# Attention on one core: unnormalised exponentials, the reciprocal sums applied after the second product, two-bank score tiles and probability transposes one head pair later

## The chip, the cores and the metric

The kernel runs on 1 core of one Trainium2 chip. Five engines work side by side, each through its own queue in program order: TensorE (PE; its weight loads are listed apart as PEld), VectorE (DVE), ScalarE (ACT), GpSimd (POOL) and SyncE (SP), from which all transfers between HBM and SBUF are issued. TensorE writes only into PSUM, which has 8 banks; the other engines carry results from there to SBUF. The metric is the device time of one execution in microseconds.

## The reference

```python
scores = scale * np.matmul(q, k.transpose(0, 1, 3, 2))      # B, H, S, D = 4, 8, 576, 64
scores = np.where(causal, -1000000000.0, scores)
a = np.exp(scores - scores.max(-1, keepdims=True))
a /= a.sum(-1, keepdims=True) + 1e-09
local = np.matmul(a, v)
q_p = np.where(q > 0, q, np.exp(q) - 1.0) + 1.0
mem_out = (q_p @ M_prev) / (q_p @ z_prev + 1e-06)           # per head
g = 1.0 / (1.0 + np.exp(-beta))                             # one gate per head
x = g * mem_out + (1 - g) * local                           # -> 2304 tokens x 512
h = x @ w_in; sp = np.log1p(np.exp(h))
x = (h * np.tanh(sp)) @ w_out                               # 512 -> 2048 -> 512
out = ((x @ w1) * (x @ w2)) @ w3 @ w_out2                   # 512 -> 1024 -> 512
```

The change touches only the attention part, and what follows directly from where its buffers lie.

## The kernel before

Attention takes two heads at a time: 4 batches of 4 pairs are 16 pairs, and the loop at L487 makes 17 rounds, as each round works on pair `p` and finishes pair `p - 1`. The 576 query rows of a pair are cut into blocks of 128; block `ib` of 0 to 3 exists once for each head (`e` of 0 and 1), and the last 64 rows of both heads share one block of 128 (`s_last`, L365).

In one round, `s_blocks` (L359) multiplies `qt` by `kt` into PSUM bank A. The two heads lie on the upper and lower 64 partitions, so each product uses 64 rows of the array (the form is shown as 64*128). `maxed` (DVE, L352) adds the mask and finds the row maximum, and `expd` (ACT, L357) takes exponentials with their row sums. `normed` (L336) forms 1/sum and multiplies each block of exponentials by 1/sum and by 1 - g, half of the blocks on DVE and half on POOL (L347). `pt_g` (L401) transposes them in 7 groups of up to four 128x128 blocks through PSUM bank F, and ACT copies each group to SBUF (L407). `pv` (L410) then adds up in PSUM bank X the memory term (`M_` times the transposed `phi`) and the products of `v` with the transposed probabilities. Here each head fills 64 columns of the array (shown as 128*64). The sum is split into a rounded high part and a remainder (ACT L427, DVE L67) and kept in `xt` for the layers that follow.

`prep_qk` (L289) transposes q and k of the next pair (5 blocks each, L286) and copies them (L292). `prep_phi` (L304) computes the feature map, its norm with `z`, scales it by g/norm (POOL L326) and transposes it (5 blocks, L330 copies). Groups 1 and 0 of the transposes of a pair are written in its own round, the other five in the next.

The inputs of the layers hold 64-bit words, two 32-bit halves each, which `decode` (L91) turns into floats with six DVE instructions (L101 to L114) and one on POOL (L119) for a tile of 128x512; two more POOL instructions split it into high and low parts (L64, L67). In rounds 2 to 11 one such tile is decoded as background: eight for the first quarter of `w_in` and `w_out` (`lq0`) and two of `pre`. In the last round the first product of the layers, `emit_h((0, 0))`, is written between the end of the attention and the rest. It is followed by the loop at L627, unit after unit: `emit_h` (48 products of 384 columns), `emit_x2` of the unit before (48 more, which need `w_out`), and `split_y`. Every fp32 product shows as two matmul instructions of the same shape.

PSUM has 3 banks for A, 3 for X and 2 for F, each handed out singly, through attention and layers alike. The order of instructions within an engine is not the order of the source: a planner with a model of instruction times orders them (`schedule_with_timeline_sim`, L752) by source order and readiness. `tc.issue_after(i)` makes what it encloses queue behind `i` on the engine of `i`.

## Time and profile before

| what | value |
|---|---|
| median of 3 runs | 1037.71 us (1035.83 to 1039.62) |
| profiled execution | 1036.43 us, span 1034.6 us |
| mean granted TensorE clock | 0.998 |
| TensorE busy, weight loads busy | 98%, 82% of the span |
| DVE, ACT, POOL busy | 59%, 49%, 33% of the span |

The span runs from the first to the last instruction; the time of the execution has some 1.8 us around it. Attention takes the first quarter of the span, the layers the rest. A busy TensorE in this profile means that some matmul was under way: the matmuls are pipelined, and the end of each is modelled. What one really costs is read from the distance between the starts of two that follow each other. The chain of waits gives such distances directly, since it lists in order of time what the end waited for. Where two heads run on different halves of the array, their instructions start together.

### The profile page before, as it was taken

Reading aid. Unit: us, or ns where it says so; the run is one execution under the profiler, and the core shown is the slowest. Engines: PE = TensorE matmul, PEld = TensorE weight load, DVE = VectorE, ACT = ScalarE, POOL = GpSimd, SP = SyncE. Lnnn points to the kernel's source line nnn. Section 1 sums busy time; section 2 is a strip of 40 time slices with the busy share of each in tenths; the row PEclk is TensorE's granted clock in tenths of the full one; section 3 lists DMA queues with packets and bytes.
Section 4 is the critical chain, followed back from the end, with each engine's and each line's share of the span. In section 5 each row is a group of like instructions: output and inputs, shape, how many; then the busy total and the mean of one; then the engine's idle time right before and its main releaser. Section 6 shows DMA issues by size and latency. Waiting matters only on the chain.

```text
span 1034.6 us, 15072 instructions
## 1 busy us (share of the span) xinstructions
PE 1014.0 (98%) x5552; PEld 847.1 (82%) x5552; DVE 615.5 (59%) x1364; ACT 505.1 (49%) x1016; POOL 337.9 (33%) x345
## 2 busy tenths in 40 slices
PE   7999999999999999999999999999989999999998
PEld 4555656556799999999999999999768888888897
DVE  5999998865279765757576666668983121121111
ACT  4777768767546665555656545442323121221212
POOL 6776675651045434252434321112550000000000
PEclk9999999999999999999999999999999999999999
DMA  6434344310133233112312456222410010100101
GB/s 150 113 95 108 95 115 110 83 41 14 61 104 122 77 107 114 49 65 99 123 41 82 153 198 220 81 73 82 152 41 1 1 41 1 42 1 0 41 1 61
DMA packets 93626, 81.73 MB, mean 79 GB/s; under 512 B 68720, under 2 KB 72816, under 8 KB 93552
## 3 DMA queue, kind: packets, MB, share of 16 engines
q1 hardware_dynamic: 93552, 80.76, 25.2%
q8 instruction: 44, 0.72, 0.3%
q14 instruction: 30, 0.25, 0.1%
HBM read 65.54 MB, written 15.20 MB: 78 GB/s over the span
## 4 chain that ended last, share of the span: by engine, by line
PE 86%; DVE 6%; ACT 3%; SPq 2%; DMA 2%; issue 1%; POOL 1%; POOLq 0%; DVEq 0%; ACTq 0%
PE psX L61 34%; PE psA L61 29%; PE psF L61 16%; PE psF L405 5%; PE psX L286 2%; SPq L268 1%; ACT y L459 1%; DVE da L105 1%; PE psF L584 1%; DVE s L347 1%; ACT L456 0%; DMA draw<-in_moe_w_dram 0%; DVE da L103 0%; DVE gl L67 0%; DMA wft<-w_dram 0%
## 5 line engine op out<-in xcount | busy, mean ns | idle before, releaser
L119 POOL TENSOR_TENSOR da<-da,draw 128x512 f32<-128x512 f32 x72 | 104.1, 1455 | 331.4 <-DVE draw L114 255.9
L61 PE MATMUL psX<-gh,wqt 128*128 128x384 f32 x768 | 196.1, 335 | 0.2
L61 PEld LDWEIGHTS psX<-gh,wqt 128*128 128x128 f32 x768 | 138.6, 188 | 1.5 <-DVE y L463 0.5
L61 PE MATMUL psX<-gl,wqt 128*128 128x384 f32 x384 | 128.3, 335 | 1.1 <-DVE gl L67 1.1
L61 PE MATMUL psA<-xt,wqt 128*128 128x384 f32 x624 | 115.0, 336 | 1.4 <-DVE y L463 1.4
L61 PEld LDWEIGHTS psA<-xt,wqt 128*128 128x128 f32 x624 | 108.5, 188 | 3.2 <-DVE y L463 1.7
L357 ACT ACTIVATE s<-s,acc 128x384 f32<-128x384 f32 (+3 forms) x144 | 85.0, 595 | 37.5 <-DVE acc L352 21.1
L61 PE MATMUL psA<-x2h,w12t 128*128 128x512 f32 (+1 forms) x288 | 81.1, 357 | 2.9 <-POOL w12t L64 2.8
L61 PE MATMUL psX<-wft,room 128*128 128x512 f32 x336 | 82.6, 390 | 0.0
L352 DVE CUSTOM_DVE_ANT_0 s<-psA,mask 128x512 f32<-128x512 f32 (+2 forms) x144 | 65.0, 477 | 19.5 <-PE psA L61 16.9
L703 ACT COPY bs<-psA 128x512 f32<-128x512 f32 (+1 forms) x40 | 21.8, 544 | 112.3 <-PE psA L61 105.7
L61 PE MATMUL psX<-pt,raw 128*64 128x64 f32 (+4 forms) x576 | 75.0, 328 | 0.0
L61 PE MATMUL psA<-kt,qt 64*128 64x384 f32 (+3 forms) x256 | 71.1, 485 | 3.7 <-DVE acc L352 3.2
L61 PE MATMUL psF<-xt,wqt 128*128 128x384 f32 x408 | 73.9, 335 | 0.0
L61 PEld LDWEIGHTS psX<-gl,wqt 128*128 128x128 f32 x384 | 72.0, 188 | 1.8 <-DVE gl L67 1.4
L61 PEld LDWEIGHTS psX<-wft,room 128*128 128x128 f32 x336 | 62.6, 188 | 12.7
L407 ACT COPY pt<-psF 128x512 f32<-128x512 f32 (+1 forms) x112 | 59.0, 544 | 26.9 <-PE psF L405 23.4
L560 DVE TENSOR_TENSOR x<-x,psX 128x384 f32<-128x384 f32 x72 | 39.6, 549 | 54.1 <-PE psX L61 53.9
L61 PEld LDWEIGHTS psF<-xt,wqt 128*128 128x128 f32 x408 | 71.0, 188 | 0.1
L471 ACT CAST gh<-y 128x768 fp32r<-128x768 f32 x48 | 40.1, 837 | 57.6 <-PE psX L61 51.5
L61 PE MATMUL psA<-x2s,w12t 128*128 128x512 f32 x288 | 67.9, 389 | 0.0
L405 PEld LDWEIGHTS psF<-ident,s 128*128 128x128 f32 x400 | 45.3, 141 | 26.1 <-ACT phi L330 10.6
(117 smaller groups left out, 1938.9 us busy)
## 6 DMA issues: line engine op xcount, KB each, us to landing
draw<-in_moe_w_dram SPq DMA_DIRECT2D x32, 512.0 KB, 3.6
draw<-in_moe_w_out_dram SPq DMA_DIRECT2D x24, 512.0 KB, 4.0
draw<-in_moe_w_in_dram SPq DMA_DIRECT2D x16, 512.0 KB, 3.9
out_dram<-ob SPq DMA_DIRECT2D x18, 256.0 KB, 2.0
raw<-in_q_dram SPq DMA_DIRECT2D x32, 128.0 KB, 2.6
raw<-in_k_dram SPq DMA_DIRECT2D x32, 128.0 KB, 3.2
raw<-in_v_dram SPq DMA_DIRECT2D x32, 128.0 KB, 2.7
o_dram<-draw SPq DMA_DIRECT2D x8, 512.0 KB, 2.9
```

Source lines behind the costliest of these rows:

```text
L61: nc.tensor.matmul(o, lhsT=l, rhs=r, start=start, stop=stop)
L105: V.tensor_scalar(out=ai, in0=ai, scalar1=3, scalar2=0x3FFFFFF8, op0=ALU.logical_shift_left, op1=ALU.bitwise_and)
L119: nc.gpsimd.tensor_tensor(out=a, in0=a, in1=lw.bitcast(F32), op=ALU.add)
L268: dm(out=a[:, 0:4, e], in_=src[b, h0 + e, 0:512, :].rearrange("(i p) d -> p i d", p=128))
L286: nc.tensor.transpose(pt[:, x:x + 128], src[:, i].rearrange("p h d -> p (h d)"), ident)
L352: nc.vector.tensor_tensor_reduce(out=s, in0=o, in1=m, op0=ALU.add, op1=ALU.min, scale=-scale, scalar=init, accum_out=a,)
L357: nc.scalar.activation(out=s, in_=s, func=AF.Exp, scale=-1.0, bias=a, accum_out=r)
L405: nc.tensor.transpose(o[:, 128 * x:128 * x + 128], src[:, 128 * jb:128 * jb + 128], ident)
L407: nc.scalar.copy(out=t[:, 0:n], in_=o[:, 0:n])
L471: nc.scalar.copy(out=gh, in_=y[i])
L560: r = nc.vector.tensor_tensor(out=d, in0=d, in1=o, op=ALU.add)
L703: nc.scalar.copy(out=bs, in_=pb)
```

## The change

The exponentials are no longer normalised before they are transposed. 1 - g multiplies `v`, and g multiplies `M_prev` (`gate_v`, `gate_m`, on POOL). The feature map is scaled by (sum + 1e-9)/norm, so that every term of the sum in PSUM lacks the same factor 1/sum. 1/sum is spread over 64 columns, transposed on TensorE beside the feature map (`scale_phi`, `trans_phi`), and DVE multiplies the finished sums by it as it takes them out of PSUM. The split into high and low parts then works from SBUF, its subtraction on POOL.

A score tile now has two banks, one for each head, and there are two of them; X has two banks, F two. All seven groups of `pt_g` of a pair lie in the next round, three of them copied by DVE. The products of `pv` queue behind the last transpose of their pair. Blocks of q, k and phi are laid out so that four transposes serve 512 rows, and the last 64 rows of both heads go through small products with parts of an identity (`tails`, and two for q). z is loaded per batch, v by itself.

Background decoding in the attention rounds is by half tiles, one in each of rounds 3 to 10, which makes the four `w_in` tiles. The four `w_out` tiles of the first quarter are decoded in the last round, and no `pre` tile is in the attention. The PSUM pool of the attention is closed behind it, and the layers open a new one with the old sizes.

```diff
+    sk = ExitStack()
+    pool = [sk.enter_context(tc.tile_pool(name="ps0", bufs=1, space=PSUM))]
+    banks = {"X": 2, "F": 2}
...
 
     def psA():
-        return bank("A")
+        return pool[0].tile([128, 2, 512], F32, tag="A", name="psA", bufs=2)
...
+        for c in range(KD + KQ):
+            w, r0, c0 = (w_in, 128 * c, FQ * g) if c < KD else (w_out, FQ * g + 128 * (c - KD), 0)
+            for h in range(0, FQ, dec["w"]):
+                cs = slice(h, h + dec["w"])
+                yield words(w, r0, c0 + h), to_split(t[:, 0, c, cs], t[:, 1, c, cs])
...
+    decoder(at, 1, 1, WN // 2)
...
+    def gate_m(b):
+        for e, hv in enumerate((UP, DN)):
+            m = mr[b % 2][hv, :, e]
+            nc.gpsimd.tensor_tensor(
+                out=m, in0=m, in1=g_[hv, 1, e::2][:, :, None].to_broadcast([64, NP, D]), op=ALU.mult
+            )
...
+    def tails(o, src):
+        for e, hv in enumerate((UP, DN)):
+            mm(o[hv], src, ident[:, 64 * e:64 * e + 64], True, True)
...
+        d = st[p]
+        qt = ep.tile([128, 512], F32, tag="qt", name="qt", bufs=2)
+        kt = ep.tile([128, S], F32, tag="kt", name="kt", bufs=2)
+        for t, nm in ((qt, "q"), (kt, "k")):
+            o = psX()
+            trans4(o, d[nm])
+            nc.scalar.copy(out=t[:, 0:512], in_=o)
+            d[nm + "t"] = t
+        o = psX()
+        for e, hv in enumerate((UP, DN)):
+            mm(o[hv, 0:128], d["q"][:, 8], idh[:, e], True, True)
+        tails(o[:, 128:192], d["k"][:, 8])
+        t4 = ep.tile([128, 128], F32, tag="qd", name="qd", bufs=2)
+        nc.scalar.copy(out=t4, in_=o[:, 0:128])
+        nc.scalar.copy(out=kt[:, 512:S], in_=o[:, 128:192])
...
+        d["e"], d["dn"] = e, dn
+
+    def gate_v(p):
+        h0 = 2 * (p % NP)
+        a = st[p]["v"]
+        nc.gpsimd.tensor_tensor(
+            out=a, in0=a, in1=g_[:, 0:1, h0:h0 + 2, None].to_broadcast([128, NB, 2, D]), op=ALU.mult
         )
...
+    def scale_phi(p):
         d = st[p]
-        og = ogp[:, p % NP]
-        sl = slice(0, 8) if len(xs) > 1 else slice(8, 9)
-        rv = d["sum"][:, sl]
-        nc.vector.tensor_scalar(out=rv, in0=rv, scalar1=1e-9, scalar2=None, op0=ALU.add)
-        nc.vector.reciprocal(out=rv, in_=rv)
-        for ib, e in xs:
-            s = s4[:, 0:S] if ib == 4 else d["s"][ib, e]
-            x = 8 if ib == 4 else 2 * ib + e
-            (nc.gpsimd if x in ON_POOL else nc.vector).tensor_scalar(
-                out=s, in0=s, scalar1=d["sum"][:, x:x + 1], scalar2=og[:, x:x + 1], op0=ALU.mult, op1=ALU.mult
-            )
+        e, dn, sm = d["e"], d["dn"], d["sum"]
+        rb = ap_.tile([128, NC, D], F32, tag="phit", name="rb", bufs=1)
+        r = ap_.tile([128, NC], F32, tag="rs", name="rs", bufs=2)
+        nc.vector.scalar_tensor_tensor(out=dn, in0=sm, scalar=1e-9, in1=dn, op0=ALU.add, op1=ALU.mult)
+        nc.vector.tensor_scalar(out=r, in0=sm, scalar1=1e-9, scalar2=None, op0=ALU.add)
+        nc.vector.reciprocal(out=r, in_=r)
+        nc.gpsimd.tensor_tensor(out=e, in0=e, in1=dn[:, :, None].to_broadcast([128, NC, D]), op=ALU.mult)
+        nc.gpsimd.tensor_copy(out=rb[:, 0:8], in_=r[:, 0:8, None].to_broadcast([128, 8, D]))
+        d["r"], d["rb"] = r, rb
+
+    def trans_phi(p):
+        d = st[p]
+        e, r = d["e"], d["r"]
+        t = ap_.tile([128, 2, S], F32, tag="phi", name="phi", bufs=1)
+        for i, x in enumerate((e, d["rb"])):
+            o = psX()
+            trans4(o, x)
+            nc.scalar.copy(out=t[:, i, 0:512], in_=o)
+        o = psF()
+        tails(o[:, 0:64], e[:, 8])
+        tails(o[:, 64:128], r[:, 8:9].to_broadcast([128, D]))
+        nc.scalar.copy(out=t[:, :, 512:S], in_=o[:, 0:128].rearrange("p (i c) -> p i c", i=2))
+        d["phi"] = t
...
-        pt = [psA() for _ in range(2)]
+        pt = psA()
...
-                mm(pt[e][:, 256 * j:256 * j + W], d["qt"][r, 128 * ib:128 * ib + 128], d["kt"][r, 0:W], True, True)
+                mm(pt[:, e, 256 * j:256 * j + W], d["qt"][r, 128 * ib:128 * ib + 128], d["kt"][r, 0:W], True, True)
...
+        s = s4[p % 2][:, 0:S]
+        pt = psA()
         for z in range(2):
-            o = psA()[:, 0:CA]
+            mm(pt[:, z, 0:CA], d["q4"], d["kt"][:, CA * z:CA * z + CA], True, True)
+        for z in range(2):
+            o = pt[:, z, 0:CA]
             cs = slice(CA * z, CA * z + CA)
...
+    BY_VECTOR = (1, 3, 5)
...
+            d["last"] = nc.tensor.transpose(
+                o[:, 128 * x:128 * x + 128], src[:, 128 * jb:128 * jb + 128], ident
+            ).ins
             d.setdefault("t", {})[ib, e, jb] = t[:, 128 * x:128 * x + 128] if e is None else (t, 128 * x)
-        nc.scalar.copy(out=t[:, 0:n], in_=o[:, 0:n])
+        if gi in BY_VECTOR:
+            nc.vector.tensor_copy(out=t[:, 0:n], in_=o[:, 0:n])
+        else:
+            nc.scalar.copy(out=t[:, 0:n], in_=o[:, 0:n])
...
-        pm, pl = psX(), psX()[:, 0:64]
...
+        pm, pl = psX(), psF()[:, 0:64]
...
+        with tc.issue_after(d["last"]):
+            mm(pm, M_.rearrange("p e d -> p (e d)"), F[:, 0:512], True, False)
+            for jb in range(4):
+                for e in range(2):
...
+        xs = ap_.tile([128, S], F32, tag="xsum", name="xsum", bufs=1)
+        nc.vector.tensor_tensor(out=xs[:, 0:512], in0=pm, in1=R[:, 0:512], op=ALU.mult)
+        nc.vector.tensor_tensor(out=xs[:, 512:S], in0=pl, in1=R[:, 512:S], op=ALU.mult)
+        x = xl[b // 2][:, :, c, S * (b % 2):S * (b % 2) + S]
+        nc.scalar.copy(out=x[:, 0], in_=xs)
+        sub(x[:, 1], xs, x[:, 0], nc.gpsimd)
...
+            if u == (0, 0):
+                if m % 2 == 0:
+                    two = psA()
+                o = two[:, m % 2, 0:CH]
...
+            lk = ExitStack()
+            decoder(lk, 2, 2, side="right")
+        if p == 0:
+            prep_phi(0)
+        if new:
+            load_v(p + 1)
+        if p + 2 < NPAIR:
+            load_pair(p + 2)
+        if now and c == 2 and b + 1 < B:
+            load_m(b + 1)
+        if now and c == 3 and b + 1 < B:
+            load_z(b + 1)
         if now:
             s_blocks(p, (3,))
+            s_blocks(p, (2,))
+        if p == 0:
+            gate_values(b_)
+            gate_m(0)
+            gate_v(0)
+        if now and c == 3 and b + 1 < B:
+            gate_m(b + 1)
         if old:
-            for i in (4, 2, 3):
+            scale_phi(p - 1)
+            for i in range(2):
+                pt_g(p - 1, i)
+        if now:
+            s_blocks(p, (0, 1))
+            s_last(p)
+        if old:
+            for i in range(2, 5):
                 pt_g(p - 1, i)
         if new:
             prep_qk(p + 1)
-        if now:
-            s_blocks(p, (2,))
-            if p == 0:
-                prep_phi(0)
-            s_blocks(p, (0, 1))
-        if p + 2 < NPAIR:
-            load_pair(p + 2)
         if old:
-            pt_g(p - 1, 5)
-            if not now:
-                run(lq0, 100)
-                split = split_y((0, 0), emit_h((0, 0)))
-            pt_g(p - 1, 6)
-        if now:
-            normed(p, [(i, e) for e in range(2) for i in range(4)])
-            pt_g(p, 1)
-        if 2 <= p < 12:
-            run(background, 1)
-        if now:
-            s_last(p)
+            for i in range(5, 7):
+                pt_g(p - 1, i)
+            trans_phi(p - 1)
+        if 3 <= p < 11:
+            run(lq0, 1)
         if old:
             pv(p - 1)
-        if now:
-            pt_g(p, 0)
         if new:
             prep_phi(p + 1)
-        if now:
-            normed(p, [(4, None)])
+            gate_v(p + 1)
+        if not now:
+            for _ in range(4):
+                run(lq0, 2)
+            split = split_y((0, 0), emit_h((0, 0)))
+    lk.close()
     at.close()
+    sk.close()
+    pool[0] = ctx.enter_context(tc.tile_pool(name="ps", bufs=1, space=PSUM))
+    banks.update(A=3, X=3)
```

## Rows read from the trace of the kernel before

**Rows 1.** Windows of three rounds: PE, PEld, DVE, ACT, POOL busy, clock, DMA, GB/s.

```profile
119.17:167.06 47.89, 47.89 (x301) 28.58 (x300) 44.08 (x124) 35.25 (x102) 32.06 (x37) 1.00 0.41 103
198.33:245.92 47.59, 47.59 (x302) 28.29 (x301) 30.36 (x105) 34.84 (x101) 18.99 (x25) 1.00 0.16 35
```

**Rows 2.** Timeline of TensorE, beginnings of two rounds: start us, us, instruction, count.

```profile
23.17 1.13 PE L61 MATMUL psA<-kt,qt 64*128 64x512 f32 x4
...
245.92 1.13 PE L61 MATMUL psA<-kt,qt 64*128 64x512 f32 x4
```

**Rows 3.** Chain of waits, 119.17 to 167.06 us: shares; then start, us, what.

```profile
by line: PE psX L61 35.3%; PE psA L61 31.4%; PE psF L405 21.2%; PE psX L286 12.4%
...
119.24 1.06 PE psA L61 x4
120.30 0.26 PE psF L405
...
124.08 0.84 PE psA L61 x2
...
129.19 0.49 PE psA L61 x2
129.68 0.55 PE psX L286 x5
...
135.19 1.05 PE psA L61 x2
...
138.31 0.73 PE psX L61 x20
...
143.66 0.86 PE psA L61 x8
```

**Rows 4.** Timeline of TensorE, second products of one pair.

```profile
130.99 1.02 PE L61 MATMUL psX<-phi,mr 128*128 128x512 f32 x2
131.94 1.07 PE L61 MATMUL psX<-pt,raw 128*64 128x512 f32 x2
132.94 0.66 PE L405 MATMUL psF<-ident,s 128*128 128x128 f32 x4
133.53 1.07 PE L61 MATMUL psX<-pt,raw 128*64 128x512 f32 x4
134.53 0.44 PE L61 MATMUL psX<-phi,mr 128*128 128x64 f32 x2
134.80 0.39 PE L286 MATMUL psX<-ident,phie 128*128 128x128 f32 x2
```

**Rows 5.** Groups by line, DVE, 23.17 to 261.77 us: busy, mean ns, idle before.

```profile
L347 DVE TENSOR_SCALAR s<-s,sum,ogp 128x384 f32<-128x384 f32 (+3 forms) x79 | 52.2, 709 | 0.9
L67 DVE TENSOR_TENSOR xt<-psX,xt 128x512 fp32r<-128x512 f32 (+1 forms) x28 | 12.7, 455 | 11.5 <-ACT xt L427 11.3
```

**Rows 6.** Timeline, first round, TensorE and DVE; idle before in brackets.

```profile
13.29 1.65 PE L61 MATMUL psA<-kt,qt 64*128 64x384 f32 x2 [2.60 <-DVE acc L352]
...
10.86 0.74 DVE L237 TENSOR_SCALAR beta<-beta 128x8 f32<-128x8 f32 x1 [4.00 <-ACT beta L236]
```

**Rows 7.** Timeline, end of the attention: ACT, DVE, POOL, TensorE.

```profile
275.17 0.49 ACT L453 ACTIVATE y<-psX 128x384 f32<-128x384 f32 x1 [1.45 <-PE psX L61]
...
279.74 0.55 DVE L463 TENSOR_TENSOR y<-y,psA 128x384 f32<-128x384 f32 x1 [11.06 <-issue]
...
281.46 0.55 DVE L463 TENSOR_TENSOR y<-y,psX 128x384 f32<-128x384 f32 x1
...
284.70 0.75 DVE L101 TENSOR_SCALAR da<-draw 128x512 int32<-128x512 int32 x2
...
288.77 1.29 DVE L114 SCALAR_TENSOR_TENSOR draw<-draw 128x512 f32<-128x512 uint32 x2
...
289.68 2.80 POOL L119 TENSOR_TENSOR da<-da,draw 128x512 f32<-128x512 f32 x2 [28.70 <-PE psX L61]
...
293.64 2.53 POOL L148 TENSOR_TENSOR draw<-da,draw 128x512 fp32r<-128x512 f32 x2
...
317.49 3.24 PE L61 MATMUL psA<-xt,wqt 128*128 128x384 f32 x17 [1.36 <-DVE y L463]
```

More of the change, by code (lines that the diff above doesn't have):

```diff
@@ L213, in fused_kernel @@
     )
+    idh = ep.tile([128, 2, 128], F32, name="idh")
+    nc.gpsimd.memset(idh, 0.0)
+    for e, hv in enumerate((UP, DN)):
+        nc.gpsimd.tensor_copy(out=idh[hv, e], in_=ident[hv])
     mask4 = ep.tile([128, CA], F32, name="mask4")
@@ L220, in fused_kernel @@
         )
-    ogp = ap_.tile([128, NP, 9], F32, name="ogp")
-    g_ = ep.tile([128, 2, H], F32, name="gates")
+    g_ = ap_.tile([128, 2, H], F32, name="gates")
+    s4 = [ap_.tile([128, 640], F32, name=f"s4{i}") for i in range(2)]
+    for t in s4:
+        nc.gpsimd.memset(t[:, S:640], 0.0)
+    qz = ep.tile([128, NC, D + 1], F32, name="qz")
+    nc.gpsimd.memset(qz[:, :, D:D + 1], 1e-6)
     mr = [ap_.tile([128, NP, 2, D], F32, name=f"mr{i}") for i in range(2)]
@@ L226, in fused_kernel, with load_z @@
         nc.gpsimd.memset(t, 0.0)
+    z = ep.tile([128, 3 * NP, D], F32, name="zr")
+    def load_z(b):
+        dm(out=z[:, 0:2 * NP], in_=z_prev[b].partition_broadcast(128))
+        for e, hv in enumerate((UP, DN)):
+            dm(out=z[hv, 2 * NP:], in_=z_prev[b, e::2].partition_broadcast(64))
     def load_m(b):
@@ L275, in load_pair @@
             t[nm] = a
-        t["z"] = ep.tile([128, 2, D], F32, tag="zr", name="zr", bufs=3)
-        dm(out=t["z"], in_=z_prev[b, h0:h0 + 2].partition_broadcast(128))
         st[p] = t
-    def trans(src, evac):
-        for c0, c1 in ((0, 256), (256, S)):
-            pt = psX()
-            for i in range(2) if c0 == 0 else (2, 3, 4):
-                x = min(128 * i, S - 128) - c0
-                nc.tensor.transpose(pt[:, x:x + 128], src[:, i].rearrange("p h d -> p (h d)"), ident)
-            evac(slice(c0, c1), pt[:, 0:c1 - c0])
@@ L289, in prep_qk, with load_v @@
[L289 to L302 removed]
+    def load_v(p):
+        b, c = divmod(p, NP)
+        h0 = 2 * c
+        a = ap_.tile([128, NB, 2, D], F32, tag="vr", name="raw", bufs=4)
+        for e in range(2):
+            dm(out=a[:, 0:4, e], in_=v[b, h0 + e, 0:512, :].rearrange("(i p) d -> p i d", p=128))
+        for hv in (UP, DN):
+            dm(out=a[hv, 4], in_=v[b, h0:h0 + 2, 512:S, :].rearrange("h p d -> p h d"))
+        st[p]["v"] = a
@@ new lines, in two, with trans4 @@
+    def two(src, i):
+        return src[:, 2 * i:2 * i + 2].rearrange("p h d -> p (h d)")
+    def trans4(o, src):
+        for i in range(4):
+            nc.tensor.transpose(o[:, 128 * i:128 * i + 128], two(src, i), ident)
+    def tails(o, src):
+        for e, hv in enumerate((UP, DN)):
+            mm(o[hv], src, ident[:, 64 * e:64 * e + 64], True, True)
+    def prep_qk(p):
+        d = st[p]
[7 more added lines that the diff above has]
+        o = psX()
+        for e, hv in enumerate((UP, DN)):
+            mm(o[hv, 0:128], d["q"][:, 8], idh[:, e], True, True)
[3 more added lines that the diff above has]
+        nc.scalar.copy(out=kt[:, 512:S], in_=o[:, 128:192])
+        d["q4"] = t4
+        d["s"] = {}
+        d["sum"] = ap_.tile([128, NC], F32, tag="sum", name="sum", bufs=2)
+        d["acc"] = ap_.tile([128, 10], F32, tag="acc", name="acc", bufs=2)
@@ L442, in emit_h @@
         for m in range(KQ):
[L443 removed]
+            if u == (0, 0):
+                if m % 2 == 0:
+                    two = psA()
+                o = two[:, m % 2, 0:CH]
+            else:
+                o = bank(HU.get(u, HT[g == NQ - 1])[m])[:, 0:CH]
             ms = slice(128 * m, 128 * m + 128)
@@ L485, in fused_kernel @@
     pre = predecode()
-    background = chain(lq0, pre)
     for p in range(NPAIR + 1):
         now, old, new = p < NPAIR, p > 0, p + 1 < NPAIR
+        b, c = divmod(p, NP)
         if old:
```

138 lines of the change are left out of this document (43 added, 95 removed).

## The prediction

> **What bounds the kernel now.** The windows come first, then the starts on TensorE, then the chain of waits, then the engines beside it. Two windows of three rounds each, both beginning and ending on the first score product of a round, take 47.89 and 47.59 us [rows 1], so 15.96 and 15.86 us a round; over fourteen rounds it is (245.92 - 23.17)/14 = 15.9 [rows 2]. In the first window DVE is busy 44.08 us, in the second, where no tile is decoded in the background, 30.36. A third of DVE's work is gone and the round is 0.1 us shorter: DVE does not set it. TensorE is busy for the whole of both, and in the chain of waits every piece of a round is TensorE's. So the round lasts as long as TensorE's own list of instructions. It is not short of work but of good order. By the shares in the chain [rows 3], of 15.96 us a round gives 31.4% or 5.01 us to scores, 35.3% or 5.63 to the second products, 21.2% or 3.38 to the transposes of the exponentials and 12.4% or 1.98 to those of q, k and phi.
>
> Two losses show in these. First, heads that don't meet: the widest scores of both heads together (four instructions) take 1.06 us, and in another round those of one head alone (two) take 1.05 [rows 3]. What is alone is doubled. The second products show the same: one head's 512 columns go from 131.94 to 132.94, the other's only from 133.53 to 134.53, behind four transposes [rows 4]. Second, changes of form: five transposes in a row take 0.55 us, 0.11 each, and a single one between two products of other forms 0.26 [rows 3]. An excursion costs some 0.15 us.
>
> **The change part by part**, for one round on TensorE.
>
> *Scores.* With two banks in one tile, both heads get their banks at the same moment. Widest block 1.06, blocks 0 and 1 of both heads 0.86 (the eight-instruction piece), the 384-wide block at most the 0.84 that one head takes alone, two products of the last block 0.49 each [rows 3]: 3.74 us against 5.01. Gain at best 1.27, at worst 0 if the planner parts the heads. I take all 1.27, because nothing that either head waits for differs any more.
>
> *Second products.* They now queue behind the last transpose of their pair, so no transpose of that pair can part the heads. Memory term 0.95 (130.99 to 131.94) and 0.27; one head's 1280 columns at 1.00 per 512 are 2.5 us [rows 4], with the other head beside it; the small products of the last block 0.73 in one piece [rows 3]. Sum 4.45 against 5.63: gain at best 1.2, at worst 0, since scores and transposes of the following pair may still come between. I take three quarters, 0.9.
>
> *Added products.* Transposes of q, k, phi and of 1/sum number 16 instead of 15: 0.11. The tails add 12 instructions of 64 columns for k, phi and 1/sum; in a row such an instruction takes 0.73/20 = 0.037 us [rows 3], so 0.45. The two 128-wide products for q are four instructions, 0.3 by twice that rate. Two more excursions are 0.3. Sum 1.2. From below it is 0.7 (no new excursion), from above 2 us, if the small groups are strewn one by one. I take 1.2.
>
> *Fewer excursions of the transposes.* 25 cost 3.38 now and 25 x 0.11 = 2.75 in a row; half of the 0.63 is taken, 0.3 (0 to 0.6).
>
> Together -1.27 - 0.9 + 1.2 - 0.3 = -1.3 us a round, between -2.4 and +2.0. I go on with -1.15, as the planner's order is not known: fifteen rounds give -17.
>
> *The other engines.* On DVE the multiplications by 1/sum go, 52.2/15 = 3.5 us a round, and the split of the sums, 12.7/14 = 0.9 [rows 5]. The split reads 576 columns out of PSUM in that 0.9, so the three copies of 512 columns that come in are put at 0.8 each, and the final multiplication, of 576 again, at 0.9. Decoding halves. DVE ends near 12 of 15 us. POOL loses its half of the normalising and gets the gate on v, the spread of 1/sum and the final subtraction, about as much. ACT gives up three of seven copies and gets wider ones for phi. All three stay under TensorE and cost nothing; if DVE were late, a copy for F (two banks) would hold the next group of transposes, up to 0.8 us each. The stall of the normalised exponentials that are needed in their own round goes too; late next is the copy of the transposed phi, which the memory term needs, and score products of the next pair can cover it. On SP a pair has 12 transfers instead of 11, and z three per batch. They lead by two pairs and are hidden.
>
> *First round.* TensorE waits 2.60 us there for DVE, and DVE has waited 4.00 us for the gate values, in front of the first maximum [rows 6]. The change places them behind two score blocks. The transposes of this round move to the last one. I take -4 (from -6 to +1; q and k come by one transfer more each, z and v lie ahead of the second pair).
>
> *End of the attention.* The last pair gains like a round, about -1, and inherits thirteen transposes, +1.4. The four `w_out` tiles now lie here: two tiles occupy DVE from 284.70 to 290.06 and POOL from 289.68 to 296.17 [rows 7], so four take some 10.5 and 13 us. DVE is idle for 11.06 and POOL for 28.70 us in that place now. That is cover for most, but the `pre` tiles and the split of the second unit queue behind on DVE, and already now TensorE waits there, for 1.36 us at 317.49. I take +2 (0 to +13). The handover of PSUM is new: if a bank of the new pool has to wait until the old one is done with, the second unit waits for the first unit's `y`, which goes from 275.17 to 282.0 [rows 7], 6.8 us. Bounds 0 and 6.8; I take +2, as products of the last pair lie beside it.
>
> Sum against the profiled execution: 1036.4 - 17 - 4 + 0.4 + 4 = 1019.8 us. That execution lies 1.3 us under the median, so the median of the changed kernel is put at 1021 us.
>
> **A rule weighed.** TensorE is busy 47.89 of 47.89 us, its weight loads 28.58 (60%), DVE 44.08 (92%) [rows 1]. The Trainium skill, "Perfetto Trace Analysis", section "Identifying the Most-Contended Engine", holds matmul busy time to be a poor measure and would go by weight loads and by the occupancy of the others; by that DVE is the engine to relieve. By that rule the change would bring more than I say (first rival below); the second window speaks against it.
>
> **The rivals.**
>
> *DVE sets the round after all.* It falls from 44.08/3 = 14.7 to about 12 us in ten rounds with decoding; with the other terms unchanged, 1036.4 - 27 - 4 + 4 and 1.3 make 1011. For it: 92% busy. Against: the round without decoding is no shorter. 0.06.
>
> *The pairing is won and spent again.* Scores gain, the second products stay parted since the planner puts scores between them, and the tails cost 1.8: -1.27 + 1.8 - 0.3 is about +0.2 a round, and 1036.4 + 3 - 4 + 0.4 + 4 + 1.3 = 1041; with the tails at 1.4 it is -0.2 a round and 1035. For it: small products stand in many pieces now. 0.16.
>
> *The end eats the gain (slower).* The `w_out` tiles come behind the exponentials and copies of the last pair, the first `emit_x2` stands without its weights, and the new PSUM pool waits for the whole old one. Price 13 + 6.8 us; with rounds at -0.5 and the start at -4 it is 1036.4 - 7.5 - 4 + 0.4 + 20 + 1.3 = 1047. It decides if the last `w_out` tile is ready later than some 18 us after the last score block, the length of the two units' 96 products (17 of them take 3.24 us [rows 7]). Against it: POOL and DVE stand idle there. 0.13.
>
> *The change doesn't do what it says.* The planner still parts the heads, and the additions stand alone: +1.3 a round, 1036.4 + 19.5 - 4 + 0.4 + 4 + 1.3 = 1058 us. For it: the order is the planner's, not the source's. 0.05.
>
> **How the numbers follow.** The forecast has 0.60; its own range goes from 1007 (rounds at -2, first round -6, end at 0) to 1032 (rounds at -0.5). The range that should hold 8 in 10 takes in the first rival and most of the second: 1004 to 1040; outside it stay the third, the fourth and the edges. A measurement tells about 0.3% or 3 us from no change. Faster by that, below 1034.6: the forecast, the first rival and some of the second, 0.72. Within: most of the second, 0.08. Slower: the rest of it, the third and the fourth, 0.20.
>
> **What would show it.** The distance from one round's widest scores to the next falls from 15.9 to about 14.7; the chain of waits shows scores in pieces of four and eight instructions, never two alone; the second products stand in one or two pieces of some 2.5 us; DVE's share falls and TensorE's stays full. New rows of 64-column products with q, k and phi stand in pairs. In the end, idle time before the first products that need `w_out` (L61, `gh`, `wqt`) or before the second unit's first product would be the third rival. The forecast is wrong if the round stays at 15.9 or above, or if TensorE shows idle time in the rounds.

## The result, and the profile after

The changed kernel takes 1050.7 us (median of 4 runs, 1048.1 to 1053.1) against 1037.1 for the kernel before beside it: ratio 1.013, 95% interval 1.009 to 1.016. It is slower by 1.3%; the forecast was 1021. The profiled execution took 1053.13 us, 1051.4 of them span.

The rounds took the time that was forecast. Three rounds of the changed kernel, the view of [rows 1] (us, then PE, PEld, DVE, ACT, POOL busy, clock, DMA share, GB/s):

```profile
146.20:190.44 44.24, 43.61 (x353) 27.97 (x352) 27.04 (x93) 31.94 (x94) 20.80 (x23) 1.00 0.29 67
```

That is 14.75 us a round (forecast 14.7, before 15.9). The chain of waits, as in [rows 3], shows both heads together in pieces of eight and twelve, and the second products in one piece of eighteen (512 columns) and one of twenty-two (the last block). It is no longer TensorE's alone: of the three rounds' chain 11.4%, or 1.7 us a round, are ScalarE's copies of transposes (L442, L371). Its shares, then pieces of one round:

```profile
by line: PE psA L62 25.3%; PE psX L62 24.7%; PE psF L435 14.7%; PE psX L298 13.2%; PE psF L62 10.0%; ACT pt L442 7.4%; ACT phi L371 4.0%; issue 0.9%
...
146.27 1.70 PE psA L62 x8
...
149.03 0.59 ACT phi L371
149.62 0.50 ACT pt L442
...
151.82 3.16 PE psX L62 x18
...
155.95 2.02 PE psA L62 x12
...
158.90 1.10 PE psF L62 x22
```

On DVE the lines of [rows 5] are gone; the copies of the transposes and the final multiplication stand there instead (busy us, mean ns, idle before):

```profile
L440 DVE COPY pt<-psF 128x512 f32<-128x512 f32 x42 | 28.8, 686 | 25.5 <-PE psF L435 25.5
...
L463 DVE TENSOR_TENSOR xsum<-psX,phi 128x512 f32<-128x512 f32 x14 | 9.6, 689 | 17.0 <-PE psX L62 17.0
```

But only rounds 7 to 14 (counted from 0, as the pairs) are like this. Rounds 2 to 6 of the same execution take 86.9 us instead of 73.7, with TensorE idle and its clock partly halved:

```profile
29.80:50.66 20.86, 15.47 (x111) 10.27 (x110) 10.10 (x37) 11.03 (x33) 11.40 (x14) 0.84 0.45 110
50.66:67.38 16.72, 14.96 (x110) 9.72 (x109) 14.63 (x44) 10.19 (x30) 9.94 (x13) 0.90 0.31 77
67.38:81.53 14.15, 13.99 (x114) 8.98 (x114) 11.06 (x39) 8.98 (x28) 7.95 (x11) 1.00 0.45 106
81.53:101.69 20.16, 16.91 (x118) 10.28 (x117) 12.08 (x39) 11.29 (x33) 9.62 (x13) 0.83 0.29 73
101.69:116.70 15.01, 14.72 (x118) 9.30 (x117) 11.82 (x43) 10.43 (x32) 10.67 (x14) 1.00 0.38 91
```

All eight background half tiles are decoded in these five rounds, although the source emits them in rounds 3 to 10: the planner moves them forward. How such a decode holds up a round shows in the timeline of round 5, where DVE stands for the tile's load, and TensorE then for a copy that DVE makes behind it (idle before in brackets):

```profile
88.21 0.47 DVE L102 TENSOR_SCALAR da<-draw 128x256 int32<-128x256 int32 x1 [3.50 <-DMA draw<-in_moe_w_in_dram]
...
89.33 1.33 PE L435 MATMUL psF<-ident,s 128*128 128x128 f32 x5 [3.18 <-DVE pt L440]
```

Still, the last pair's widest scores begin at 234.68 us, 11.2 ahead of [rows 2]. Not all of this lead is time saved. Rounds 1 to 4 hold 58, 111, 110 and 114 instructions of TensorE where rounds from the seventh on hold 119, and what they lack comes at the end: from the last pair's widest scores to the 192nd product of the layers TensorE has 448 instructions, in the kernel before 378. Behind those scores the whole lead is lost. The timeline of the end of attention and of a later unit of the layers:

```profile
252.68 0.43 DVE L102 TENSOR_SCALAR da<-draw 128x512 int32<-128x512 int32 x1 [3.31 <-DMA draw<-in_moe_w_out_dram]
...
260.15 0.76 PE L435 MATMUL psF<-ident,s 128*128 128x128 f32 x5 [1.65 <-DVE pt L440]
...
271.05 0.65 PE L435 MATMUL psF<-ident,s 128*128 128x128 f32 x4 [1.73 <-DVE xsum L464]
...
288.80 0.43 DVE L102 TENSOR_SCALAR da<-draw 128x512 int32<-128x512 int32 x1 [5.69 <-DMA draw<-in_moe_w_out_dram]
...
335.12 1.01 PE L62 MATMUL psX<-gh,wqt 128*128 128x384 f32 x2 [3.83 <-DVE x L622]
```

DVE stands for the loads of tiles, or in a decode step (one of 1.41 us ends at 259.50, just before the copy that TensorE waits for at 260.15); copies and sums wait behind it, and TensorE waits for those. Against [rows 7], DVE's first decode step after attention comes 4.1 us later (288.80 against 284.70). At the 192nd product of the layers the changed kernel is 2.2 us behind (308.2 against 306.0), and behind the stall that ends at 335.12 it is 5.4 (348.0 against 342.6 at the 384th product, 547.7 against 542.3 at the 1536th). The other 11.4 us of the 16.8 between the two spans go in and behind the last quarter, where `fold` transposes w3 and multiplies it with `w_out2` into one weight for the last stage: its transposes run from 619.2 to 745.7 us, before from 596.3 to 719.2. Behind it the last stage lacks its weights; from 719 to 800 us TensorE is idle for 10.6 us, before for 5.2:

```profile
759.37 1.06 PE L62 MATMUL psX<-wft,room 128*128 128x512 f32 x3 [2.91 <-ACT wft L800]
```

### The profile page after: what moved, and what is told of

Same layout as the page of the kernel before. It is cut to its first block, busy times and chain, and to the rows that moved or that the text cites. A ratio compares the mean times of both kernels' runs of the same rounds, so it can differ in the third digit from the quotient of the medians.

```text
span 1051.4 us, 15583 instructions
## 1 busy us (share of the span) xinstructions
PE 1001.1 (95%) x5824; PEld 850.6 (81%) x5824; DVE 588.1 (56%) x1319; ACT 487.1 (46%) x968; POOL 329.0 (31%) x337
## 4 chain that ended last, share of the span: by engine, by line
PE 73%; DVE 11%; DMA 5%; ACT 3%; POOL 3%; issue 2%; SPq 2%; POOLq 0%; DVEq 0%; ACTq 0%
PE psX L62 26%; PE psA L62 25%; PE psF L62 17%; PE psF L435 3%; PE psX L298 2%; DMA draw<-in_moe_w_dram 2%; POOL da L120 1%; DVE da L109 1%; DVE da L104 1%; DVE da L106 1%; DMA draw<-in_moe_w_in_dram 1%; DVE draw L115 1%; DVE da L102 1%; DVE draw L113 1%; ACT pt L442 1%
## 5 line engine op out<-in xcount | busy, mean ns | idle before, releaser
L120 POOL TENSOR_TENSOR da<-da,draw 128x512 f32<-128x512 f32 (+1 forms) x76 | 104.0, 1378 | 360.3 <-DVE draw L115 335.3
L62 PE MATMUL psA<-xt,wqt 128*128 128x384 f32 x648 | 119.2, 336 | 0.0
L62 PEld LDWEIGHTS psA<-xt,wqt 128*128 128x128 f32 x648 | 113.4, 189 | 0.3
L384 ACT ACTIVATE s<-s,acc 128x512 f32<-128x512 f32 (+2 forms) x144 | 83.4, 582 | 34.9 <-DVE acc L379 34.9
L435 PE MATMUL psF<-ident,s 128*128 128x128 f32 x400 | 68.2, 298 | 12.7 <-DVE pt L440 6.3
L62 PE MATMUL psF<-xt,wqt 128*128 128x384 f32 x408 | 73.7, 334 | 0.4 <-DVE xsum L464 0.4
L62 PEld LDWEIGHTS psA<-x2h,w12t 128*128 128x128 f32 x288 | 52.7, 193 | 13.5 <-POOL w12t L65 3.7
L102 DVE TENSOR_SCALAR da<-draw 128x512 int32<-128x512 int32 (+1 forms) x76 | 33.9, 462 | 52.4 <-PE psF L648 17.7
L62 PEld LDWEIGHTS psA<-x2s,w12t 128*128 128x128 f32 x288 | 54.1, 188 | 11.2
```

The lines of the kernel that those rows point to most:

```text
L62: nc.tensor.matmul(o, lhsT=l, rhs=r, start=start, stop=stop)
L102: V.tensor_scalar(out=ai, in0=hw, scalar1=0x7FFFFFFF, scalar2=None, op0=ALU.bitwise_and)
L120: nc.gpsimd.tensor_tensor(out=a, in0=a, in1=lw.bitcast(F32), op=ALU.add)
L384: nc.scalar.activation(out=s, in_=s, func=AF.Exp, scale=-1.0, bias=a, accum_out=r)
L435: d["last"] = nc.tensor.transpose(o[:, 128 * x:128 * x + 128], src[:, 128 * jb:128 * jb + 128], ident).ins
```

## Experiments

Times are medians, and ratios are to the kernel before, run on the same chip, with their 95% intervals. Differences in us are between medians that can come from different chips, on which the kernel before took 1035.7 to 1038.7; where that matters, the ratios are compared.

**Tiles of the last stage.** `pre_early`:

```diff
                 run(nextq if n < 4 else chain(islice(nextq, 1), islice(pre, 1)), 2)
+                if g in (1, 2) and n == 3:
+                    run(pre, 1)
```

> The changed kernel, with two more of the sixteen background tiles of the last stage's weights decoded in the second and third quarter of the layers (one each beside the fourth unit), so that none is left for the start of the last quarter. Theory A (the two tiles that no longer fit in attention hold back the folding of w3, and that delays the last quarter): the first w3 load lands near 588 us instead of 613, the last products of the folding end near 725 instead of 749, and the time falls by 20 to 25 us, to 1026 to 1031. Theory B (the loss is the TensorE's waits and the half clock in attention and at its end): 1050, within 3 us. Theory C (the new PSUM layout of the layers costs): 1050 too.

Measured: 1041.5, ratio 1.004 (1.002 to 1.005), 9.3 us below the changed kernel. The time of w3's transposes (the view by line, first and last start):

```profile
L648 PE MATMUL psF<-ident,da x64: 270/272/273, 598.5 to 720.7; 128*128 128x128 f32 x64
```

The place of theory A holds, its size was too large: `fold` comes back by 21 to 25 us (4.2 of them lie ahead of the layers' 192nd product already, where the two kernels' source does not differ), but its own products then stand in the last quarter again instead of behind it (from the 1536th product of the layers to the last it takes 183.2 us instead of 171.5), so 9 are gained. The counter-test in the old kernel, `before_late_pre`, makes the two tiles late there:

```diff
-    background = chain(lq0, pre)
+    background = lq0
```

> The kernel before, with only the first quarter's eight tiles decoded in attention; the two tiles that followed them there go to the start of the last quarter, as in the changed kernel. Theory A: the folding ends some 24 us later and the time rises by 20 to 25 us, to 1057 to 1062, with attention unchanged to 1 us. Theories B and C: 1037, within 3 us.

Measured: 1049.1, ratio 1.011 (1.010 to 1.013), 11.8 us slower, attention unchanged (last pair's scores at 246.3 us). So this one displacement costs 9 to 12 us in either kernel; theories B and C alone fall.

**Decodes in the rounds, by emission.** `late_decode` and, for the end, `last_copies_act`:

```diff
-        if 3 <= p < 11:
+        if 7 <= p < 15:
...
-        if gi in BY_VECTOR:
+        if gi in BY_VECTOR and p < NPAIR - 1:
```

> The changed kernel, with the background half tiles decoded in rounds 7 to 14 instead of 3 to 10. Theory B1 (VectorE stands at the head of its queue for the load of such a tile in the early rounds, score and copy work waits behind it, and TensorE with it, whose clock then falls): rounds 2 to 6 come down from 20.8, 16.7, 14.2, 20.2 and 15.0 us to 14.8 each, no half clock between 43 and 95 us, the last pair's scores start near 222 instead of 234.7 us, and the time falls by 10 to 13 us, to 1037 to 1041. Rival B2 (the early rounds wait for the loads of q, k and v themselves, which share the queue): rounds 2 to 6 stay above 16 us on the mean, the time falls by under 4 us. If the layers' last quarter is set by the folding alone (theory A), the gain at the end of attention still goes through, because the folding's loads move with it.

> The changed kernel, with the last pair's three probability copies of VectorE on ScalarE instead, because at the end of attention VectorE also decodes w_out tiles and waits for their loads. Theory B (these copies queue behind waiting decodes): the last TensorE waits of 1 to 2 us for them between 260 and 276 us go, no half clock at 272 to 279 us, and the time falls by 3 to 8 us. Rival: ScalarE has the split of y and the copies of phi in the same stretch, so it becomes late itself: within 2 us of 1050.

Measured: 1051.3 (1.010 to 1.016) and 1050.9 (1.012 to 1.016), both nothing. The first told nothing: the planner decoded the first half tile at 41 us all the same, and rounds 2 to 6 stayed at 86.8 us. In the second TensorE waited for ScalarE's copies instead (1.17 and 1.51 us in the places of 1.73 and 1.19), and the stretch from the first unit of the layers to the second took 34.9 us instead of 35.5.

**Decodes held by an edge on VectorE.** `pinned_decode` and `all_in_rounds` (the latter with all sixteen half tiles, two a round from the eleventh on); `mark` is the round's last maximum, in `s_last`:

```diff
-            run(lq0, 1)
+            with tc.issue_after(st[p]["mark"]):
+                run(lq0, 1)
```

> The changed kernel, with the background half tiles of rounds 3 to 10 ordered on VectorE behind the last score step of their own round. (In the run late_decode they were only emitted later, and the planner still put the first at 41 us, before the work that waits behind it.) Theory B1 (VectorE stands at the head of its queue for a tile's load while the finished sums and copies wait behind it): rounds 2 to 6, together 86.9 us in the changed kernel, come down to 74 to 78 us, no half clock between 43 and 95 us, the time falls by 8 to 13 us, to 1038 to 1043. Rival B2 (the loads of q, k and v of the first rounds are what is late): rounds 2 to 6 stay above 82 us together and the time falls by under 4 us.

> The same order, and all sixteen half tiles in rounds 3 to 14 (two a round from the eleventh on), so that no w_out tile is left for the end of attention. Theory B (the end of attention loses its time to VectorE, which decodes four tiles there and waits for their loads 3.3 and 1.3 us): beyond pinned_decode, the stretch from the last pair's widest scores to the second unit of the layers, 48.5 us in the changed kernel, comes down to 39 to 42 us, and the time falls by a further 6 to 10 us, to 1029 to 1036; rounds 11 to 14 stay within 0.3 us of 14.75, since VectorE has 5.7 us free in a round and a half tile costs it 2.0. Rival (the stretch is long because one whole pair's transposes and second products are behind, and ScalarE's copies set it): 46 us or more, and the time moves by under 3 us against pinned_decode.

Measured: 1049.5 (1.010 to 1.014) and 1056.6 (1.015 to 1.020). Rounds 2 to 6 came down to 79.8 us, but rounds 5 to 11, each behind a half tile, took 15.6 us instead of 14.75. Rounds 13 and 14 of `all_in_rounds`, which got more than one half tile with one raw buffer, took 19.8 and 20.6; the end of attention did shrink, from 48.5 to 43.5 us between the last pair's scores and the second unit. And round 2, now without any decode, still took 20.3. Its timeline in `pinned_decode`:

```profile
29.73 1.25 POOL L348 TENSOR_TENSOR raw<-raw,gates 128x640 f32<-128x640 f32 x1 [6.03 <-DMA raw<-in_v_dram]
...
36.12 1.25 POOL L348 TENSOR_TENSOR raw<-raw,gates 128x640 f32<-128x640 f32 x1 [3.77 <-DMA raw<-in_v_dram]
...
38.05 0.76 DVE L333 SCALAR_TENSOR_TENSOR phie<-phie,phit 128x576 f32<-128x576 f32 x1 [4.54 <-POOL phit L332]
...
42.27 0.76 DVE L341 TENSOR_REDUCE dn<-qz 128x9 f32<-128x585 f32 x1 [2.86 <-POOL qz L339]
...
33.05 1.30 SPq L290 DMA_DIRECT2D raw<-in_v_dram  x2
...
44.77 1.11 PE L437 MATMUL psF<-ident,s 128*128 128x128 f32 x4 [4.51 <-DVE xsum L466]
```

This is to be read from the end: TensorE waits for the finished sums, these stand on DVE behind the reduction of `qz`, that waits for POOL, and POOL has stood 6.0 and 3.8 us for v tiles, whose transfers SP issues last, 1.30 us for two. The gate on v is new on POOL, so the lead of the loads, enough for TensorE's use of v, isn't enough for POOL's.

**Loads of v.** `v_on_act` issues v of the first four pairs, and M, from ScalarE's queue:

```diff
+        dv = nc.scalar.dma_start if p < 4 else dm
         for e in range(2):
-            dm(out=a[:, 0:4, e], in_=v[b, h0 + e, 0:512, :].rearrange("(i p) d -> p i d", p=128))
+            dv(out=a[:, 0:4, e], in_=v[b, h0 + e, 0:512, :].rearrange("(i p) d -> p i d", p=128))
```

> The changed kernel, with the loads of v of the first four pairs and of the two M tiles issued from ScalarE's queue instead of SyncE's. In pinned_decode the TensorE still stood 4.5 us at 40 us with no decode near: GpSimd waits 6.0 and 3.8 us for v tiles that SyncE issues last of some 0.55 us each, and VectorE stands behind GpSimd. Theory D (the new multiply of v and M by the gates puts late loads at the head of GpSimd's queue, and VectorE's scores stand behind it): round 2 falls from 20.8 to 15 to 17 us, and the time by 4 to 6 us, to 1044 to 1047. Rival (round 2 waits for its decode, which stays here, or for q and k, whose loads now only come sooner): round 2 stays above 19 us and the time within 2 us of 1050.

Measured: 1051.6 (1.013 to 1.016). Round 2 fell to 14.6 us, as theory D says, but the planner put two half tiles each into rounds 5 and 6, which took 20.0 and 20.9. The loss had moved.

**The place on VectorE's queue.** `decode_gap` (`mark` is the reciprocal of the sums) and `decode_free_slot` (`mark` is the third of VectorE's copies, of group 5):

```diff
-            run(lq0, 1)
+            with tc.issue_after(st[p - 1]["mark"]):
+                run(lq0, 1)
```

> The changed kernel, with each background half tile ordered behind the reciprocal of the sums of its round (rounds 3 to 10), where VectorE is free for 1.6 us, instead of behind the last score step (pinned_decode, 15.63 us a round against 14.75 without a decode). Theory E (a half tile costs 0.88 us in a round by the place in VectorE's queue, since it delays the reciprocal, and the transposes with it, not by VectorE's load): rounds 4 to 9 take 14.75 to 15.0 us, and the time falls by 5 to 8 us against pinned_decode, to 1042 to 1045. Rival (VectorE is the bound of a round with a decode, or the buffers are): rounds stay at 15.5 or more and the time near 1049.

> The changed kernel, with each background half tile ordered behind the third copy that VectorE makes of a pair's transposes (rounds 3 to 10). In decode_gap the same steps, behind the reciprocal, took 1.23, 1.41 and 1.23 us instead of 0.28, each ending with a GpSimd instruction that ran beside it, and the rounds 18 to 20.4 us. Theory F (a decode step of VectorE that meets GpSimd at work waits for its end; in the changed kernel GpSimd's new products lie beside VectorE's short gaps; between 138.7 and 143 us of a round GpSimd is idle): the six steps take 0.28 to 0.42 us each, rounds 4 to 10 take 14.75 to 15.0 us, rounds 2 to 10 together 137 to 141 us against 145.9 in the changed kernel, the time 1042 to 1046. Rival (VectorE's queue cannot take a half tile in any place without a loss of about 0.9 us): those rounds at 15.6 or more, the time 1049 or more.

Measured: 1070.7 (1.027 to 1.035) and 1041.4 (1.002 to 1.004): 29 us between two places for the same six instructions. The timeline of one round in `decode_gap`:

```profile
116.38 1.15 POOL L360 TENSOR_TENSOR phie<-phie,dn 128x576 f32<-128x576 f32 x1 [1.79 <-DVE rs L358]
117.49 1.49 POOL L68 TENSOR_TENSOR xt<-xsum,xt 128x576 fp32r<-128x576 f32 x1
119.59 1.44 POOL L348 TENSOR_TENSOR raw<-raw,gates 128x640 f32<-128x640 f32 x1 [0.61 <-DMA raw<-in_v_dram]
...
116.45 1.23 DVE L102 TENSOR_SCALAR da<-draw 128x256 int32<-128x256 int32 x1
117.71 1.41 DVE L104 TENSOR_SCALAR da<-da 128x256 f32<-128x256 f32 x1
...
119.94 1.23 DVE L113 TENSOR_SCALAR draw<-da 128x256 int32<-128x256 int32 x1
...
122.29 1.10 PE L435 MATMUL psF<-ident,s 128*128 128x128 f32 x8 [3.35 <-DVE pt L440]
```

and the same steps in `decode_free_slot`, where POOL has nothing between 141.25 and 145.11 us:

```profile
142.23 0.28 DVE L102 TENSOR_SCALAR da<-draw 128x256 int32<-128x256 int32 x1
142.55 0.29 DVE L104 TENSOR_SCALAR da<-da 128x256 f32<-128x256 f32 x1
...
143.67 0.29 DVE L113 TENSOR_SCALAR draw<-da 128x256 int32<-128x256 int32 x1
```

Each long step ends 0.14 to 0.15 us behind a POOL instruction (117.68 and 117.53, 119.12 and 118.98, 121.17 and 121.03). So the steps seem to have met POOL at work and waited for its end. The Trainium skill, "SBUF — State Buffer", section "SBUF: two separate sides", has it that GpSimd and a VectorE instruction that runs in a mode with two ports, or has two inputs in SBUF while GpSimd reads SBUF, exclude each other from a shared pair of ports for a whole instruction. These rows agree in the waiting; in which mode the steps run, no run here shows. In `pinned_decode` one step stood likewise: in each of the rounds of 15.6 us the last step took 1.52 to 1.54 us instead of 0.42 (80.34 to 81.86, a POOL instruction ended at 81.57).

The waiting is a part of the loss and not all of it. In rounds 5 to 10 of `decode_gap` the six steps of a half tile took 3.9 to 5.1 us instead of 2.0 to 2.9, but a round took 3.3 to 5.7 us more than 14.75; the rest, that copies stand behind the steps in this place, was not measured apart. In `decode_free_slot`, from round 5 on, a round took 14.48 or 14.75 us, with or without a decode.

**First units of the layers.** `spread_pre` takes the two extra tiles away from the first unit and adds one, two and one beside the fourth unit of three quarters:

```diff
-            if u == (0, 0):
-                run(pre, 2)
...
+                if n == 3:
+                    run(pre, 2 if g == 1 else 1)
```

> The changed kernel, with none of the last stage's tiles decoded right behind the end of attention beyond the regular two: one, two and one tile beside the fourth unit of the first three quarters instead, so that none is left for the last quarter either. Theory G (the two extra tiles start late at the end of attention, 288.8 us against 284.7 before, VectorE runs behind and TensorE stands 4.2 us at 331 us for its copies, at half clock behind that): beyond pre_early's gain of 9 us, the stretch from the seventh to the ninth block of 48 products, 23.2 us, comes down to 16.7, and the time to 1033 to 1037. Rival (the stall moves to the next unit with the tiles): 1040 to 1043, as pre_early.

Measured: 1039.2, ratio 1.000 (0.999 to 1.002). The stretch with the stall that ends at 335.12 (4.2 us from start to start; products 288 to 384 of the layers) fell from 23.1 to 16.7 us, as theory G says. Of these 6.4 us 2.1 come back later (products 1152 to 1536 take 68.6 us against 66.5 in `pre_early`). That leaves 4.3; the medians differ by 2.3 us from `pre_early`, but they come from two chips, and by the ratios it is 0.36%, 3.7 us give or take 2.0.

**Together.** `all_repairs` (all_in_rounds and pre_early), `all_repairs_2` (v_on_act, decode_gap with a second half tile behind the finished sums in rounds 11 to 14, two raw buffers, pre_early) and `all_repairs_3` (v_on_act; decode_free_slot with fourteen half tiles in rounds 2 to 15, two raw buffers; spread_pre):

> all_in_rounds with the two late background tiles decoded in the second and third quarter as in pre_early. If the three losses are separate, their gains add: 9 us of pre_early on top of all_in_rounds, 1020 to 1027, faster than before by 1 to 1.6%. If they overlap (the folding waits for the same loads, or the clock falls elsewhere), 1030 or more.

> Four repairs together: v and M from ScalarE's queue; the sixteen half tiles all in attention, one a round behind the reciprocal in rounds 3 to 14 and a second behind the finished sums in rounds 11 to 14, with two raw buffers; no w_out tile left for the end; two tiles more of the last stage in the second and third quarter. If the losses are those of theories A, D and E and of the end of attention (9 for the late tiles, 5 for round 2, 6 for the decodes' place, 5 for the end), 1025 to 1031, faster than before by 0.6 to 1.2%. If a round with two half tiles still takes over 17 us, 1035 or more.

> Four repairs together: v and M of the first rounds from ScalarE's queue; fourteen of the sixteen half tiles behind the third VectorE copy of rounds 2 to 15, with two raw buffers, and one w_out tile left for the end of attention; the last stage's tiles as in spread_pre. If theories A, D, F and G hold and the end of attention gains by its three tiles fewer: rounds 2 to 6 together 74 to 77 us, time 1008 to 1020, faster than before by 1.5 to 2.8%. If it stays above 1035, the losses are elsewhere.

Measured: 1044.3 (1.006 to 1.008), 1074.5 (1.035 to 1.039), and 1016.9, ratio 0.980 (0.978 to 0.982). The first two carried a bad place for the decodes along. The third beats both kernels. Its windows, rounds 2 to 6, and the end of attention from the first unit of the layers to the second:

```profile
31.20:101.70 70.50, 69.22 (x568) 44.69 (x567) 52.25 (x174) 52.77 (x157) 40.28 (x47) 1.00 0.39 90
...
231.30:260.30 29.00, 25.55 (x206) 19.78 (x204) 17.76 (x38) 17.03 (x35) 11.67 (x15) 1.00 0.07 19
```

In the changed kernel the same 206 instructions of TensorE took 35.5 us:

```profile
247.70:283.20 35.50, 28.49 (x206) 21.00 (x204) 26.86 (x48) 16.73 (x33) 20.37 (x17) 0.90 0.18 60
```

From this version `repairs_v_on_sp` takes the loads of v and M back to SP, and `repairs_pv_parted` takes away the edge that holds the second products behind the last transposes (`with tc.issue_after(d["last"])`):

> all_repairs_3 with the loads of v and M back on SyncE's queue. Theory D (late v tiles at the head of GpSimd's queue stretch round 2): round 2 at 19 to 21 us instead of 13.3, the time up by 4 to 7 us, to 1021 to 1024. Rival (v_on_act did not lower the time by itself, 1051.6 against 1050.7, so the place of these loads is worth nothing): 1017, within 2 us.

> all_repairs_3 without the edge that holds the second products behind the last transposes of their pair, so that the planner may put them between the transposes again. Forecast's theory (the second products in one block are worth 0.9 us a round): rounds of 15.2 to 15.6 us instead of 14.48 and 14.75, the time up by 8 to 14 us, to 1025 to 1031. Rival (the planner keeps them together anyhow, or the transposes fill the gaps): rounds within 0.3 us, the time within 4 us of 1017.

Measured: 1023.1 (0.983 to 0.986) and 1049.5 (1.008 to 1.012). So the place of v's loads is worth 6.2 us (round 2 is back at 21.1), and the edge 32.6: rounds of 16.2 to 17.9. The planner strews the transposes among the second products, and TensorE then also stands for the finished sums on DVE, 11.2 us in rounds 5 to 14, where `all_repairs_3` has no such wait. A part of one round in `repairs_pv_parted`:

```profile
147.54 0.66 PE L436 MATMUL psF<-ident,s 128*128 128x128 f32 x4 [1.25 <-DVE xsum L465]
...
149.69 1.04 PE L436 MATMUL psF<-ident,s 128*128 128x128 f32 x8
150.66 1.07 PE L62 MATMUL psX<-pt,raw 128*64 128x512 f32 x2
151.66 0.66 PE L299 MATMUL psX<-ident,raw 128*128 128x128 f32 x4
152.16 0.60 PE L436 MATMUL psF<-ident,s 128*128 128x128 f32 x4
152.69 1.07 PE L62 MATMUL psX<-pt,raw 128*64 128x512 f32 x4
```

**The two-bank tile.** `single_banks` gives the changed kernel four single banks again:

```diff
-        return pool[0].tile([128, 2, 512], F32, tag="A", name="psA", bufs=2)
+        return bank("A")
...
-        pt = psA()
+        pt = [psA() for _ in range(2)]
```

> The changed kernel with its two-bank score tiles undone: every score block has a tile of one bank for each head, four single banks instead of two pairs. Theory (the rounds' gain of 1.15 us comes largely from the pairing of the heads): rounds 7 to 14 rise from 14.75 to 15.6 to 16.2 us, the scores' pieces appear one head at a time again, and the time rises by 10 to 16 us. Rival (the pairing follows from the order of the round, with the transposes a pair behind, and the tile's shape adds nothing): rounds stay within 0.3 us of 14.75 and the time within 3 us of 1050.

Measured: 1056.6 (1.0165 to 1.020), 5.9 us slower than the changed kernel; rounds of 15.28 us from the eighth on, and among the blocks of 128 and 256 columns the heads are parted in two pieces of four (0.92 us each) where the pair takes 0.93 for all eight. The widest blocks stay paired. Between theory and rival: the tile is worth 0.53 us a round, about half of what was expected.

## Why the prediction was wrong

**Rounds: the sum right, in part by luck.** -1.15 us each was forecast, -1.15 came (15.9 to 14.75) in every round without a decode. By the chain, scores take 1.70 + 2.02 = 3.72 us (forecast 3.74) and the second products 3.16 + 1.10 = 4.26 (4.45 at best): 0.5 us more gained there than the 0.9 that was taken. The small products of q, k, phi and 1/sum take 0.48 + 0.38 = 0.86, less than the 1.2. Against that, the transposes of the exponentials, put at -0.3, came at +0.6 with what they wait for: 2.2 us of their own (3.38 before), and 1.8 in which the chain stands, nearly all of it on ScalarE's copies. What shorter copies would give was not tried. The two edits are not worth what their terms say either: undone alone, the tile gives 0.53 instead of 1.27. The edge behind the transposes gives 2.4 instead of 0.9 (from round 5 on, mean 16.97 in `repairs_pv_parted` against 14.61 in `all_repairs_3`), of which 1.1 are the wait for the finished sums; the parted products are in the other 1.2. The first round gained 2.8 us (20.40 against 23.17 [rows 2]), forecast 4. The rival that DVE's busy time sets the round did not come in: that time fell from 10.1 us a round without decodes [rows 1] to 9.0, the round with the order of TensorE's work.

**"All three stay under TensorE and cost nothing": the step that failed.** DVE's sum was right, even high: 9.0 us a round without a decode, copies 0.69 instead of 0.8, the final multiplication 0.91 as put. But an engine that is busy 61% still costs time by what stands at the head of its queue. With the score maxima, three copies and both final multiplications of a round on DVE, and two F and two X banks, any step that waits there for a load or for POOL keeps banks from TensorE. Decodes that were hidden in the kernel before (0.1 us a round between the two windows of [rows 1]) cost 0.9 us each in `pinned_decode` and 3.3 to 5.7 in rounds 5 to 10 of `decode_gap`; in the changed kernel it is 9.3 us in all by `decode_free_slot`.

**"They lead by two pairs and are hidden", said of SP's loads: failed.** They lead for TensorE, not for the new gate on POOL: 6.2 us by `repairs_v_on_sp`.

**End of attention, -1 + 1.4, "+2 (0 to +13)" and +2: mis-sized.** From a lead of 11.2 us to 2.2 behind at the 192nd product is a loss of 13.4, and 4.4 was the sum. The stretch of 206 instructions takes 35.5 us and comes down to 29.0 with three tiles fewer there and the clock whole: about 6.5. Another 4.0 are work put off from the first rounds, where the forecast had 0.4: even in `all_repairs_3` TensorE is busy for 62.9 us from the last pair's widest scores to the 192nd product, before for 58.9. That the handover of PSUM costs anything, no trace shows: the second unit follows the last pair after 0.40 us. It was not tried alone.

**The two `pre` tiles: left out of the sum.** I let them "queue behind on DVE" at the seam and did not follow them to their end: they take the last places in the layers, `fold` starts 23 us later and the last stage stands. 9.3 us by `pre_early`, 11.5 by `spread_pre`, which takes a stall of the first units away with them.

9.3 + 6.2 + 11.5 are 27.0 of the 33.8 us between the changed kernel and `all_repairs_3`; the remaining 6.8 fit the 6.5 of the end of attention. By the ratios it is 10.4 + 5.2 + 13.0 of 34.2. These parts were measured in different kernels; that they add up fits, and is not shown. The rival "the end eats the gain" had the sign and, at 1047, nearly the time, but not the cause: its late `w_out` tiles and its PSUM pool make up under a quarter of the loss (6.5 of 33.8). What stays open is the end of attention: its 6.5 us were taken away only together with other repairs.

## What to carry to other kernels

When a change shifts evictions or products to an engine that "has time", look at the head of its queue, not at its sum: which loads, which other engine's end will it stand for, and which banks wait behind it. Follow every moved background job to its last consumer, even 300 us later. And hold such jobs by an edge at a place where their neighbours are idle; emitting them later moves nothing if a planner orders the work.

## What the hardware showed beside this

A decode step that takes 0.43 us in the round before (`v_on_act`, 87.39) took 3.18 at 98.32 us, beside three POOL instructions in a row (97.99 to 101.22), and ended 0.28 us behind the third. That fits a wait for all of them and not only for the one at work when it came. And a stall costs twice: behind the idle stretches of 36 to 43 us in the changed kernel, in which TensorE was busy 4.02 of 7.30 us, the granted clock is 0.50, the 1.2 GHz level:

```profile
36.00:43.30 7.30, 4.02 (x45) 3.10 (x43) 2.24 (x5) 0.16 (x2) 5.32 (x7) 1.00 0.64 155
43.30:50.10 6.80, 4.69 (x24) 3.84 (x25) 4.56 (x20) 5.32 (x17) 3.17 (x5) 0.50 0.23 65
```

In the kernel before this level appears only up to 22.4 us and at 729 to 732; in the changed kernel in seven places behind 43 us, and in `all_repairs_3` the mean is back at 0.995.
